# Attention with a mixture of experts: binding the first sequence's transposes, value products and early expert products behind its scores

## The chip, the cores and the metric

The kernel runs on one core of a Trainium2 chip. The metric is the device time of one execution in microseconds (us); the median of three runs stands for a kernel.

## The reference

Four sequences of 576 tokens with eight heads of 64 columns go through causal attention with a bias that decays along the sequence; the result is the input of a mixture of eight experts, whose gate is balanced in eight rounds over all tokens.

```python
scores = scale * np.matmul(q, k.transpose(0, 1, 3, 2))
cum = np.cumsum(np.maximum(s, 0.0), axis=-1)
bias = -(cum[:, :, :, None] - cum[:, :, None, :])
scores = np.where(causal, -1000000000.0, scores + np.minimum(bias, 0.0))
attn = np.exp(scores - np.max(scores, axis=-1, keepdims=True))
attn = attn / (np.sum(attn, axis=-1, keepdims=True) + 1e-09)
x = np.matmul(attn, v)                  # tokens x 512
...
P = np.exp(x @ w_gate - max)            # then 8 rounds of row and column balancing
for e in range(E):
    out += P[:, e:e + 1] * (np.maximum(x @ w1[e], 0.0) @ w2[e])
```

## The kernel before, in words

The work has two parts. The first, which the change touches, is attention; expert 0's products run between its pieces. The second, from some 340 us on, is the other seven experts, whose products are made from sums of blocks (lines 1017 to 1236).

All values are kept as a rounded high part and a remainder, so most products are made of three matmuls.

Attention goes by pairs of heads: sequence 0 has pairs 0 to 3 (heads 0 to 7), sequence 1 pairs 4 to 7, and so on. A pair has five blocks of queries, so a step of the main loop (line 722) is one pair g and one block i; sequence 0 has steps 0 to 19. The list `slots` (line 673) holds them. The work of a step is spread over four turns of the loop:

- `st0` (line 519): the scores (two matmuls into a bank, line 505, for each of the pair's heads), the search for the largest on VectorE (line 514), the exponential with its sum on ScalarE (line 546). Three banks hold scores.
- `st1` (line 555), one turn later: a small addition on ScalarE (line 561), the reciprocal on VectorE (line 565), the scaling on ScalarE (line 568).
- `st2` (line 570), two turns later: transposes on TensorE (lines 577 and 587, two banks), copies to `at` or `al` on VectorE (lines 582, 585, 588).
- `st3` (line 591), three turns later, but for blocks 0 and 1 together after block 1 and for blocks 2 to 4 together after block 4: the product with V on TensorE (line 607, one bank `pv`), its rounding on ScalarE (line 623) and its remainder on VectorE (line 624) into `xh`, the input of the experts.

The operands of a head are made by `prep_head` (line 410) from transfers of `load_head` (line 330): the high part of Q on GpSimd (line 425), that of K and a copy of Q's on VectorE (lines 426 and 429), the remainders on GpSimd (line 432 for K, line 436 for Q, in two pieces for an odd head), the rows of the bias by transfers (lines 418 and 421). Four sets of Q operands are used in turn, so head h waits for the scores of head h - 4. V of a pair is loaded by `load_v` (line 490) into two tiles used in turn.

Expert 0's weights are split on ScalarE and GpSimd (lines 110 and 111). Its products for a sequence (`g1_half`, line 141, matmuls at line 149, each half over two of the four pairs' columns; `g2_chunk`, line 170) and the gate (`gate`, line 628, matmuls at line 632) are queued two turns after the sequence's last step (line 775), and `fill` (line 696) spreads them over the next turns. Two banks `g` hold them.

The order of the program is not that of the chip's queues: a scheduler with a timeline of its own decides, engine by engine, which of the traced instructions comes next, earlier traced ones first among those that it believes to be ready. The products with V have a priority that lets them pass 4000 places (line 606). `tc.issue_after(x)` adds an edge for the instructions in its block that are on the engine of x: they stand behind x in that engine's queue. It adds no wait on a semaphore. On the chip each engine takes its queue in order.

The main loop's part that the change touches reads:

```python
for ti in range(NS + 3):
    if ti < NS:
        ...
            st0(slots[ti], j)
    if 1 <= ti <= NS:
        st1(slots[ti - 1])
    fill(ti)
    if 3 <= ti:
        pg, pi = slots[ti - 3]
        if pi == 1:
            st3(pg, (0, 1))
        elif pi == 4:
            st3(pg, (2, 3, 4))
    for j in range(2):
        if 2 <= ti < NS + 2 and j in heads(slots[ti - 2]):
            st2(slots[ti - 2], j)
```

Of the kernel before, what the change touches and what calls it, by code (L numbers as in the profile page):

```python
# [14 lines left out]
P = 128  # L15
B, H, S, D = 4, 8, 576, 64
# [7 lines left out]
KD = DM // P  # L24
# [21 lines left out]
def fused_kernel(ctx: ExitStack, tc: tile.TileContext, qT, kT, v, s, w_gate, wu, out):  # L46
    nc = tc.nc
# [10 lines left out]
    wg = const.tile([P, KD, 16], F32R, name="wg")  # L58
# [19 lines left out]
    def xcols(b, hl, k, n0, n):  # L78
        return xgroup(b)[:, hl, k, n0 - GB[b] : n0 - GB[b] + n]
# [55 lines left out]
    gps = {}  # L135
    chunk = {}

    def bank():
        return cur["g"].tile([P, 512], F32, name=cur["gt"], tag=cur["gt"])

    def g1_half(b, u, n0, n, f, half):
        w1 = wts[u, "w1"]
        if half == 0:
            gps[0] = bank()
        ps = gps[0]
        for k in (0, 1) if half == 0 else (2, 3):
            o = k * FU + f * P
            for t, (w, x) in enumerate(((0, 0), (0, 1), (1, 0))):
                nc.tensor.matmul(  # L149
                    ps[:, :n],  # L150
                    lhsT=w1[:, w, o : o + P],
                    rhs=xcols(b, x, k, n0, n),
                    start=(k == 0 and t == 0),
                    stop=(k == KD - 1 and t == 2),
                )
        if half == 1:
            hh = hpool.tile([P, TP], F32R, name="hh", tag="hh")
            hl = hpool.tile([P, TP], F32R, name="hl", tag="hl")
            nc.scalar.activation(hh[:, :n], ps[:, :n], AF.Relu)
            nc.vector.scalar_tensor_tensor(  # L160
                out=hl[:, :n],
                in0=ps[:, :n],
                scalar=0.0,
                in1=hh[:, :n].bitcast(F32),
                op0=ALU.max,
                op1=ALU.subtract,
            )
            hts[u, n0, f] = hh, hl
# [225 lines left out]
    for n in range(4):  # L394
        qa = apool.tile([P, QW], F32R, name=f"qa{n}")
# [10 lines left out]
        vtt.append(vt)  # L406

    ops = {}

    def prep_head(h):  # L410
        rq, rk = raws.pop((h, "q")), raws.pop((h, "k"))
        ka = apool.tile([P, S], F32R, name="ka", tag="ka", bufs=4)
        kb = apool.tile([D + 4, S], F32R, name="kb", tag="kb", bufs=4)
        qa, qb = qas[h % 4], qbs[h % 4]
        rows = crow_d[h : h + 1]
        at = [(0, 0, S)] if h % 2 == 0 else [(0, 0, S - D), (S - D, S, D)]
        for i, o, n in at:
            nc.sync.dma_start(
                out=qb[D : D + 4, o : o + n].bitcast(F32), in_=rows[:, 2:6, i : i + n]
            )  # L420
        nc.sync.dma_start(out=kb[D : D + 4, :].bitcast(F32), in_=rows[:, 0:4, :])
        top = D if h < H else P
        low = slice(0, D) if h < H else slice(D, P)
        for i, o, n in at:
            nc.gpsimd.tensor_copy(qa[:top, o : o + n], rq[:top, i : i + n])
        nc.vector.tensor_copy(ka, rk)
        if h < H:
            for i, o, n in at:
                nc.vector.tensor_copy(qb[:D, o : o + n], rq[:D, i : i + n])
        else:  # L430
            nc.sync.dma_start(out=qb[:D].bitcast(F32), in_=qa[:D].bitcast(F32))
        nc.gpsimd.tensor_tensor(
            out=kb[:D], in0=rk[:D], in1=ka[:D].bitcast(F32), op=ALU.subtract
        )
        for i, o, n in at:
            nc.gpsimd.tensor_tensor(
                out=qa[D:, o : o + n], in0=rq[low, i : i + n],
                in1=qa[low, o : o + n].bitcast(F32), op=ALU.subtract,
            )
        ops[h] = (ka, kb)  # L440

    def first_heads():
# [56 lines left out]

    Ts, sums, ats = {}, {}, {}  # L500

    def scores(out, h, i, cols, first, last):
        ka, kb = ops[h]
        for n, (q, k) in enumerate(((qas[h % 4], ka), (qbs[h % 4], kb))):
            nc.tensor.matmul(  # L505
                out,
                lhsT=queries(q, h, i),
                rhs=k[:, cols],
                start=(first and n == 0),
                stop=(last and n == 1),  # L510
            )
# [58 lines left out]
    def st2(t, j):  # L570

        g, i = t
        T = Ts.pop((t, j))
        nb = min(i + 1, 4)
        tr = psa.tile([P, 512], F32, name="tr", tag="tr", bufs=2)
        for c in range(nb):
            nc.tensor.transpose(  # L577
                tr[:, c * P : (c + 1) * P], T[:, c * P : (c + 1) * P], ident
            )
        if i < 4:  # L580
            at = apool.tile([P, 512], F32, name="at", tag="at", bufs=6)
            nc.vector.tensor_copy(at[:, : nb * P], tr[:, : nb * P])
        else:
            at = apool.tile([P, 5 * P], F32, name="al", tag="al", bufs=1)
            nc.vector.tensor_copy(at[:, : 4 * P], tr)
            tr = psa.tile([P, 512], F32, name="tr", tag="tr", bufs=2)
            nc.tensor.transpose(tr[:, :P], T[:, S - P : S], ident)
            nc.vector.tensor_copy(at[:, 4 * P :], tr[:, :P])
        ats[t, j] = at
# [38 lines left out]
    def gate(b, n0, n):  # L628
        ps = bank()
        for k in range(KD):  # L630
            for x in range(2):
                nc.tensor.matmul(  # L632
                    ps[:16, :n],
                    lhsT=wg[:, k, :],
                    rhs=xcols(b, x, k, n0, n),
                    start=(k == 0 and x == 0),
                    stop=(k == KD - 1 and x == 1),
                )
        lt = apool.tile([16, 384], F32, name="lt", tag="lt", bufs=2)
        nc.scalar.copy(lt[:, :n], ps[:16, :n])  # L640
        lts[n0] = lt
# [31 lines left out]
    slots = [(g, i) for g in range(B * NPAIR) for i in range(5)]  # L673
# [48 lines left out]
    for ti in range(NS + 3):  # L722
        if ti < NS:
            g, i = slots[ti]
            if i == 4 and g + 1 < NG:
                load_v(g + 1)
            for j in heads(slots[ti]):
# [3 lines that stand above are left out]
        fill(ti)  # L731
        if 3 <= ti:
            pg, pi = slots[ti - 3]
            if pi == 1:
                st3(pg, (0, 1))
            elif pi == 4:
                st3(pg, (2, 3, 4))
        for j in range(2):
            if 2 <= ti < NS + 2 and j in heads(slots[ti - 2]):
                st2(slots[ti - 2], j)  # L740
            if j == 0:
                fill(ti)
        if ti < NS and i in (1, 3) and g + 1 < NG:
            h = 2 * (g + 1) + i // 2
            prep_head(h)
            ahead = {2: (4, 5), 3: (6,), 16: ()}.get(h, (h + (3 if h < 16 else 2),))
            for hh in ahead:
                if hh < B * H:
                    load_head(hh)
        gs = (ti - 7) // 5  # L750
        if ti >= 7 and slots[ti - 7][1] == 4 and gs >= NPAIR:
            spill(*divmod(gs, NPAIR))
        if ti in (24, 28, 32, 36):
            spill(0, (ti - 24) // 4)
        if ti == 6:
            gate_weights()
        if 4 <= ti < 18:
            u, r = divmod(ti - 4, 7)
            if r in (0, 3):
                with tc.issue_after(heads_in[0].ins):  # L760
                    w_load_early(u, (r // 3,))
            if r > 2:
                w_split_early(u, r - 3)
        prep(ti)
        if ti == 66:
            for i in range(2):
                nc.gpsimd.tensor_copy(
                    xgroup(3)[:, i, :, : EDGE[1] - EDGE[0]],
                    xgroup(2)[:, i, :, GB[3] - GB[2] : GB[3] - GB[2] + EDGE[1] - EDGE[0]],
                )  # L770

        for bb in range(B):
            if ti == (bb + 1) * 20 + 2:
                if bb < B - 1:
                    for k in range(4):
                        stream.add_visit(4 * bb + k, w_load_early, w_split_early)
                else:
                    stream.flush()
                for x, (n0, n) in enumerate(EARLY[bb]):
                    at = 4 * x + 1 if bb < B - 1 else 3 * x + 1  # L780
                    stream.queue.insert(at, lambda b=bb, n0=n0, n=n: gate(b, n0, n))
                    stream.queue.insert(at + 2, lambda n0=n0, n=n, t=bb == B - 1: gate_t(n0, n, t))
# [457 lines left out]
    k = 0  # L1240
# [107 lines left out]
    for i in range(len(steps2)):  # L1348
# [6 lines left out]
        idx, o = steps2[i]  # L1355
# [46 lines left out]
```

## Time and profile before

| | |
|---|---|
| median of 3 runs | 1686.53 us (1685.39 to 1687.65) |
| the profiled execution | 1686.63 us |
| its span, first to last instruction | 1684.8 us |
| TensorE busy | 1661.1 us (99%) |
| VectorE, ScalarE, GpSimd busy | 1177.9, 833.9, 872.9 us |
| mean granted clock of TensorE | 0.994 of 2.4 GHz |

The profile is one execution on the chip. Its engines are PE (TensorE), PEld (TensorE's loads of weights), DVE (VectorE), ACT (ScalarE), POOL (GpSimd) and SP (the queue that issues most transfers). L505 is line 505 of the kernel. A row of the instructions in order of time gives the start, the duration, the engine, the line, what it writes and reads, and in brackets how long the engine was idle before it and what ended that. Matmuls overlap, and a record's end is modelled, so a busy TensorE is not always one at its peak.

### The profile page before, as it was taken

What the parts mean: (1) busy time and instruction counts of PE and PEld (TensorE: products, weight loads), DVE (VectorE), ACT (ScalarE), POOL (GpSimd) and SP (SyncE); (2) the same over time, 40 slices, a digit from 0 to 9 for tenths busy, and PEclk for the clock granted to TensorE, in tenths of its full rate; (3) what the DMA queues carried; (4) which work ended last, traced back from release to release, by engine and by line L of the source; (5) the groups of instructions that cost most, each with busy time, mean ns of one, the idle gap of its engine ahead of it and who ended that gap; (6) DMA issues with size and microseconds to landing.
All of it is one profiled execution on the core that took longest, in us unless ns stands there. A gap on an engine that the chain in (4) does not pass through costs nothing.

```text
span 1684.8 us, 31220 instructions
## 1 busy us (share of the span) xinstructions
PE 1661.1 (99%) x11149; PEld 1565.7 (93%) x11149; DVE 1177.9 (70%) x2313; ACT 833.9 (49%) x1816; POOL 872.9 (52%) x800
## 2 busy tenths in 40 slices
PE   7999999999999999999999999999999999999999
PEld 5789898988898999999899999999999999999998
DVE  7866566655866766676457777777777777777666
ACT  5976666533544444444235444444445444444443
POOL 7857867432654554454214544554554555455544
PEclk8999999999999999999999999999999999999999
DMA  6577666284876866875956666565687666666552
GB/s 181 166 203 229 205 174 198 86 310 162 297 246 215 281 214 210 286 227 180 349 181 208 187 184 191 187 189 183 191 316 248 203 188 189 187 187 184 189 186 88
DMA packets 203578, 348.88 MB, mean 207 GB/s; under 512 B 20832, under 2 KB 102752, under 8 KB 203392
## 3 DMA queue, kind: packets, MB, share of 16 engines
q1 hardware_dynamic: 202944, 345.98, 64.2%
q8 instruction: 88, 1.44, 0.4%
q10 hardware_dynamic: 480, 0.92, 0.2%
q14 instruction: 66, 0.54, 0.1%
HBM read 247.71 MB, written 94.81 MB: 203 GB/s over the span
## 4 chain that ended last, share of the span: by engine, by line
PE 91%; DVE 5%; ACT 2%; issue 1%; DMA 1%; SPq 1%; POOL 0%; ACTq 0%; DVEq 0%; POOLq 0%
PE c L1038 34%; PE zz L1159 13%; PE zz L1216 13%; PE y L1216 10%; PE g L149 4%; PE g L178 4%; PE sc L505 3%; PE pv L607 3%; PE tr L577 2%; PE c L149 2%; PE c L178 2%; DVE s L1013 1%; DVE h L253 1%; PE g L632 0%; DVE z L256 0%
## 5 line engine op out<-in xcount | busy, mean ns | idle before, releaser
L253 POOL TENSOR_TENSOR w2o<-r,w2o 128x512 fp32r<-128x512 f32 x192 | 276.7, 1462 | 279.4 <-ACT w2o L1196 274.9
L1216 PE MATMUL zz<-w2o,h 128*128 128x256 f32 x2016 | 272.9, 280 | 0.0
L1038 PE MATMUL c<-xS,w1o 128*128 128x384 f32 x1344 | 271.7, 336 | 1.1 <-ACT t L1053 0.6
L1216 PEld LDWEIGHTS zz<-w2o,h 128*128 128x128 f32 x2016 | 263.3, 188 | 0.4 <-DVE h L253 0.2
L1159 PE MATMUL zz<-w2p,h 128*128 128x512 f32 x1008 | 256.8, 391 | 0.4 <-ACT h L1001 0.4
L1002 DVE SCALAR_TENSOR_TENSOR h<-z,h 128x384 fp32r<-128x384 f32 x252 | 193.0, 772 | 66.2 <-ACT h L1001 63.6
L1001 ACT ACTIVATE h<-z 128x384 fp32r<-128x384 f32 x252 | 130.6, 525 | 207.1 <-DVE z L256 203.3
L1038 PEld LDWEIGHTS c<-xS,w1o 128*128 128x128 f32 x1344 | 227.3, 188 | 2.9 <-DVE z L256 1.6
L1013 DVE SCALAR_TENSOR_TENSOR s<-z,s 128x384 f32<-128x384 f32 x224 | 180.7, 844 | 65.7 <-ACT s L1076 62.7
L253 POOL TENSOR_TENSOR h<-s,h 128x384 fp32r<-128x384 f32 x112 | 138.2, 1242 | 163.2 <-ACT h L1009 162.4
L1159 PEld LDWEIGHTS zz<-w2p,h 128*128 128x128 f32 x1008 | 187.0, 188 | 29.6 <-ACT h L1001 0.7
L1038 PE MATMUL c<-x,w1o 128*128 128x384 f32 x1008 | 203.0, 336 | 0.0
L1216 PE MATMUL y<-w2o,h 128*128 128x256 f32 x1512 | 201.5, 280 | 0.4 <-DVE a L1142 0.3
L1216 PEld LDWEIGHTS y<-w2o,h 128*128 128x128 f32 x1512 | 194.5, 188 | 1.0 <-DVE a L1142 0.5
L256 DVE TENSOR_TENSOR z<-c,t 128x384 f32<-128x384 f32 x252 | 136.6, 549 | 69.4 <-PE c L1038 65.3
L1038 PEld LDWEIGHTS c<-x,w1o 128*128 128x128 f32 x1008 | 170.5, 188 | 0.6
L1142 DVE SCALAR_TENSOR_TENSOR a<-zz,prob,a 128x256 f32<-128x256 f32 (+1 forms) x210 | 110.5, 529 | 67.6 <-PE zz L1216 53.0
L1009 ACT CAST h<-s 128x384 fp32r<-128x384 f32 x224 | 110.9, 513 | 74.7 <-DVE s L1013 69.7
L1038 PE MATMUL c<-xS,wp 128*128 128x384 f32 x672 | 134.6, 336 | 1.4 <-DVE z L256 1.3
L1196 ACT CAST w2o<-r 128x1024 fp32r<-128x1024 f32 x98 | 102.5, 1047 | 51.9 <-PE y L1216 41.0
L1038 PEld LDWEIGHTS c<-xS,wp 128*128 128x128 f32 x672 | 118.9, 188 | 10.0 <-DVE z L256 3.1
L253 POOL TENSOR_TENSOR wp<-s,wp 128x512 fp32r<-128x512 f32 x56 | 80.4, 1436 | 82.3 <-ACT wp L928 70.5
(151 smaller groups left out, 2723.0 us busy)
## 6 DMA issues: line engine op xcount, KB each, us to landing
w1o<-w1d SPq DMA_DIRECT2D x392, 256.0 KB
w1d<-wp SPq DMA_DIRECT2D x84, 512.0 KB
r<-wu SPq DMA_DIRECT2D x70, 512.0 KB
r<-w2d SPq DMA_DIRECT2D x56, 512.0 KB
sa<-wu SPq DMA_DIRECT2D x28, 512.0 KB
w2d<-sb SPq DMA_DIRECT2D x56, 256.0 KB
wraw<-wu SPq DMA_DIRECT2D x20, 512.0 KB
xS<-xd_S SPq DMA_DIRECT2D x12, 768.0 KB
```

The source lines that it names most:

```text
L149: nc.tensor.matmul(ps[:, :n], lhsT=w1[:, w, o : o + P], rhs=xcols(b, x, k, n0, n), start=(k == 0 and t == 0), stop=(k == KD - 1 and t == 2),)
L253: (eng or nc.gpsimd).tensor_tensor(out=out, in0=a, in1=b, op=ALU.subtract)
L256: (eng or nc.gpsimd).tensor_tensor(out=out, in0=a, in1=b, op=ALU.add)
L1001: mark["a"] = nc.scalar.activation(t[:, 0], z, AF.Relu)
L1002: mark["v"] = nc.vector.scalar_tensor_tensor(out=t[:, 1], in0=z, scalar=0.0, in1=t[:, 0].bitcast(F32), op0=ALU.max, op1=ALU.subtract,)
L1009: nc.scalar.copy(t[:, 0], z)
L1013: nc.vector.scalar_tensor_tensor(out=out, in0=z, scalar=0.0, in1=other, op0=ALU.max, op1=op)
L1038: mm = nc.tensor.matmul(ps, lhsT=w[:, wl, k], rhs=x[:, xl, k], start=(fresh and k == 0 and t == 0), stop=(k == 1 and t == 2), skip_group_c ...
L1142: nc.vector.scalar_tensor_tensor(out=a, in0=ps, scalar=prob[:, c, e : e + 1], in1=a, op0=ALU.mult, op1=ALU.add)
L1159: mm = nc.tensor.matmul(zb[ci], lhsT=h[:, a, ci * P : (ci + 1) * P], rhs=w[:, b_], start=(ui == 0 and f == 0 and t == 0), stop=(ui == UPE ...
L1196: nc.scalar.copy(w[:, :, 0], r)
L1216: nc.tensor.matmul(ps, lhsT=h[:, a, ci * P : (ci + 1) * P], rhs=w[:, ui, b_], start=(fresh and ui == 0 and t == 0), stop=(ui == UPE - 1 an ...
```

## The change

Three kinds of instructions get an edge in their engine's queue; nothing is computed otherwise.

- In turns 1 to 20, the transposes of step ti - 2 and the product with V of step ti - 3 stand behind the last score of step ti - 1 on TensorE.
- For the first sequence, expert 0's first products and the gate's products stand behind the last score of step 18 on TensorE.
- On GpSimd, the copies of Q (line 425) of heads 3 to 8 stand behind the last subtraction (line 436) of the head before.

```diff
+    def behind_first(b):
+        st = ExitStack()
+        if b == 0:
+            st.enter_context(tc.issue_after(last_score[slots[18]].ins))
+        return st
+
@@ g1_half
-            for t, (w, x) in enumerate(((0, 0), (0, 1), (1, 0))):
-                nc.tensor.matmul(
...
+            with behind_first(b):
+                for t, (w, x) in enumerate(((0, 0), (0, 1), (1, 0))):
+                    nc.tensor.matmul(
...
@@ prep_head
-        for i, o, n in at:
-            nc.gpsimd.tensor_copy(qa[:top, o : o + n], rq[:top, i : i + n])
+        with ExitStack() as st:
+            if h - 1 in split_q:
+                st.enter_context(tc.issue_after(split_q[h - 1].ins))
+            for i, o, n in at:
+                nc.gpsimd.tensor_copy(qa[:top, o : o + n], rq[:top, i : i + n])
...
-            nc.gpsimd.tensor_tensor(
+            lo = nc.gpsimd.tensor_tensor(
...
+        if h < H:
+            split_q[h] = lo
@@ scores
+    last_score = {}
+
+    def behind_scores(ti):
+        st = ExitStack()
+        if 0 < ti <= 20:
+            st.enter_context(tc.issue_after(last_score[slots[ti - 1]].ins))
+        return st
+
...
-            nc.tensor.matmul(
+            last_score[h // 2, i] = nc.tensor.matmul(
                 out,
@@ gate
+                with behind_first(b):
+                    nc.tensor.matmul(
...
@@ main loop
             pg, pi = slots[ti - 3]
-            if pi == 1:
-                st3(pg, (0, 1))
-            elif pi == 4:
-                st3(pg, (2, 3, 4))
+            with behind_scores(ti):
+                if pi == 1:
+                    st3(pg, (0, 1))
+                elif pi == 4:
+                    st3(pg, (2, 3, 4))
...
-                st2(slots[ti - 2], j)
+                with behind_scores(ti):
+                    st2(slots[ti - 2], j)
```

## Rows read from the trace of the kernel before

**Rows 1.** The page, busy time, share of the span and count of each engine.

```profile
PE 1661.1 (99%) x11149; PEld 1565.7 (93%) x11149; DVE 1177.9 (70%) x2313; ACT 833.9 (49%) x1816; POOL 872.9 (52%) x800
```

**Rows 2.** Busy time by stretch: length, engines' busy time (instructions), TensorE's clock, transfers.

```profile
core 0: us, PE busy (x) PEld busy (x) DVE busy (x) ACT busy (x) POOL busy (x), PEclk, DMA share, GB/s
0.00:42.00 42.00, 29.87 (x179) 24.84 (x179) 30.28 (x83) 22.41 (x64) 30.70 (x51) 0.81 0.68 180
42.00:84.00 42.00, 39.69 (x372) 32.75 (x372) 34.32 (x137) 40.81 (x126) 33.59 (x35) 0.95 0.58 165
84.00:126.00 42.00, 42.00 (x371) 37.54 (x371) 27.12 (x88) 32.20 (x92) 21.57 (x22) 1.00 0.71 205
```

**Rows 3.** The same view, columns as above, from 26.5 to 81.2 us.

```profile
26.50:33.60 7.10, 5.18 (x57) 4.37 (x56) 3.07 (x6) 0.04 (x2) 5.79 (x5) 0.76 0.84 237
33.60:41.60 8.00, 4.84 (x27) 3.59 (x27) 7.68 (x25) 7.14 (x24) 5.39 (x7) 0.88 0.53 146
...
56.60:69.40 12.80, 11.81 (x119) 9.45 (x118) 11.18 (x45) 12.20 (x38) 11.88 (x13) 1.00 0.58 158
69.40:81.20 11.80, 10.96 (x117) 9.21 (x115) 10.58 (x42) 11.48 (x37) 7.42 (x9) 1.00 0.72 204
```

**Rows 4.** Who waited for whom, first 200 us: total us, times, longest us.

```profile
ACT xh L623 <- PE pv L607: 9.1, 4, 7.1
```

**Rows 5.** TensorE's instructions in order of time, 25 to 90 us.

```profile
27.29 0.63 PE L577 MATMUL tr<-ident,T 128*128 128x128 f32 x4 [0.54 <-DVE at L582]
...
29.63 1.34 PE L607 MATMUL pv<-al,vt 128*64 128x64 f32 x20 [0.47 <-DVE al L588]
30.75 2.76 PE L607 MATMUL pv<-at,vt 128*64 128x128 f32 x28
33.44 0.33 PE L505 MATMUL sc<-ka,qa 128*128 128x128 f32 x1
...
41.59 0.45 PE L505 MATMUL sc<-ka,qa 128*128 128x128 f32 x1 [2.92 <-DVE mn L514]
...
78.72 1.70 PE L607 MATMUL pv<-at,vt 128*64 128x128 f32 x28
...
85.21 1.60 PE L149 MATMUL g<-xh,w 128*128 128x256 f32 x12
```

**Rows 6.** GpSimd's instructions in order of time, around 23 us.

```profile
22.80 0.88 POOL L425 CAST qa<-rx 64x576 fp32r<-64x576 f32 x1
23.76 1.70 POOL L436 TENSOR_TENSOR qa<-rawq,qa 64x512 fp32r<-64x512 f32 x2
```

**Rows 7.** ScalarE's instructions in order of time, 15 to 38 us.

```profile
15.69 0.90 ACT L568 ACTIVATE T<-T,rec 128x256 f32<-128x256 f32 x2
...
34.25 0.40 ACT L546 ACTIVATE T<-T,mn 128x128 f32<-128x128 f32 x1 [0.32 <-DVE mn L514]
34.56 0.19 ACT L546 ACTIVATION_READ_ACCUMULATOR T<-T,mn 128x1 f32 x1
...
34.78 0.29 ACT L561 ACTIVATE sm<-sm,guard 128x2 f32<-128x2 f32 x1
34.98 0.49 ACT L546 ACTIVATE T<-T,mn 128x256 f32<-128x256 f32 x1
...
37.61 0.68 ACT L568 ACTIVATE T<-T,rec 128x128 f32<-128x128 f32 x2
```

**Rows 8.** SP's queue in order of time, around 35 us.

```profile
35.28 0.41 SPq L495 DMA_DIRECT2D vt<-v  x1
```

**Rows 9.** TensorE's busy time (instructions) in one stretch: line 149, then line 632.

```profile
26.50:61.50 35.00, 1.71 (x6) 1.19 (x6) 0.85 0.59 170
...
26.50:61.50 35.00, 0.63 (x4) 0.38 (x4) 0.85 0.59 170
```

**Rows 10.** VectorE's instructions in order of time, 23 to 85 us.

```profile
23.62 0.43 DVE L426 CAST ka<-rx 128x576 fp32r<-128x576 f32 x1
...
38.44 2.08 DVE L426 CAST ka<-rawk 128x576 fp32r<-128x576 f32 x1
...
84.44 0.21 DVE L624 TENSOR_TENSOR xh<-pv,xh 128x64 fp32r<-128x64 f32 x1
```

More of the change, by code (lines that the diff above doesn't have):

```diff
@@ L147, in g1_half @@
             o = k * FU + f * P
-            for t, (w, x) in enumerate(((0, 0), (0, 1), (1, 0))):
-                nc.tensor.matmul(
[L150 to L155, printed above, removed]
+            with behind_first(b):
+                for t, (w, x) in enumerate(((0, 0), (0, 1), (1, 0))):
+                    nc.tensor.matmul(
+                        ps[:, :n],
+                        lhsT=w1[:, w, o : o + P],
+                        rhs=xcols(b, x, k, n0, n),
+                        start=(k == 0 and t == 0),
+                        stop=(k == KD - 1 and t == 2),
+                    )
         if half == 1:
@@ L408, in fused_kernel @@
     ops = {}
+    split_q = {}
     def prep_head(h):
@@ L631, in gate @@
             for x in range(2):
[L632 to L638, printed above, removed]
+                with behind_first(b):
+                    nc.tensor.matmul(
+                        ps[:16, :n],
+                        lhsT=wg[:, k, :],
+                        rhs=xcols(b, x, k, n0, n),
+                        start=(k == 0 and x == 0),
+                        stop=(k == KD - 1 and x == 1),
+                    )
         lt = apool.tile([16, 384], F32, name="lt", tag="lt", bufs=2)
```

## The prediction

> **What bounds it now.** I read the page's totals first, then busy time by stretch, then who waited for whom, then each engine's instructions in order of time around the largest wait. TensorE is busy for 1661.1 of 1684.8 us [rows 1], so all that another order can win is the 23.7 us in which it is not, and what a lower clock costs. The first 42 us hold 42.00 - 29.87 = 12.13 us of that and the next 42 us 42.00 - 39.69 = 2.31 us; from 84 to 126 us there is none, at a clock of 1.00 [rows 2]. So the change, which touches the first sequence's attention, works in the one stage that has much to give, and behind about 84 us TensorE is full: what is won or lost before is handed on to the end, and what is moved across that line is paid in full.
>
> Up to about 81 us ScalarE and VectorE set the pace. From 56.6 to 81.2 us ScalarE is busy for 12.20 of 12.80 and 11.48 of 11.80 us, VectorE for 11.18 and 10.58 [rows 3]. Against that stands the stretch from 26.5 to 33.6 us: ScalarE is busy for 0.04 of 7.10 us, VectorE for 3.07 [rows 3]. The list of waits names it: ScalarE's longest, 7.1 us, is for the product with V [rows 4]. The order on TensorE shows why. It does the transposes of step 4 from 27.29 us, then 20 and 28 instructions of the product with V for steps 2 to 4 (29.63 to 33.5 us), and only at 33.44 us the score of head 3 for step 5 [rows 5]. That score could have gone earlier: GpSimd's last piece of head 3 (the subtraction at 23.76 us, 1.70 us long) is over at 25.46 us [rows 6]. So scores that feed the two pacing engines stand in line behind 3.9 us of products that nobody needs yet. No measurement of this kernel tells a difference under 0.2% (3.4 us) from none.
>
> **The change part by part.**
>
> Steps bound behind scores. Step n's transposes must follow the scores of step n+1, and the product with V of steps 2 to 4 must follow the scores of step 6. I went through TensorE's order of the first sequence with this rule; it is broken in one place only, by the transposes of step 4 and the 48 products behind them [rows 5]. Elsewhere the binding asks for what is there. Here the score of step 5 (head 3) and both of step 6 come ahead of the 48 products. TensorE reaches them at about 27.3 us, 1.8 us after head 3 is complete, so it needn't wait for it. ScalarE then has work in its gap: exponentials of 0.40, 0.49 and 0.49 us, three reads of a sum at 0.19, two small additions at 0.29, scalings of 0.68 and 0.90 us [rows 7], together 4.1 us. These ten overlap by 0.09 us each (the first begins at 34.25 us, lasts 0.40 us, and the next begins at 34.56 us), which leaves 3.2 us. Step 7's first score should pass as well, since TensorE otherwise stands still before the products (0.47 us before 29.63 us, 0.54 us before 27.29 us [rows 5]); that is one exponential more, 0.6 us by the next larger size after 0.40 and 0.49 us, an estimate. I take 3.8 us, close to what the binding secures, because the products keep their priority and will follow closely. Bounds: all 7.1 us of the gap, if the scores up to step 9 pass too; nothing, if VectorE, which has copies and casts of its own until 29.6 us, serves the early scores no sooner than now. TensorE has room: its gaps are 1.92 us in the first stretch, then 3.16, 0.99 and 0.84 us in the others, 6.91 us together [rows 3].
>
> What the moved instructions drag along. The 48 products move back by four to six score instructions (0.33 us for the one at 33.44 us [rows 5]), under 2 us. ScalarE's rounding and VectorE's remainder of them move too; their reader, expert 0's product, comes 50 us later: nothing. On SP's queue the load of V for pair 2 waits for the last of these products and is issued at 35.28 us [rows 8], with the rows of head 6 behind it. Those wait for the last score of pair 1 anyway; without that cover the loads are up to 2 us late, for scores 20 us away: nothing.
>
> GpSimd's chain (for heads 3 to 8, the copy stands behind the last subtraction of the head before). Now head 4's copy (22.80 us, 0.88 us) goes ahead of head 3's subtraction [rows 6]; it will go behind it. Head 3 is complete 0.9 us earlier, which counts for nothing, as TensorE arrives at 27.3 us. Heads 4 and 5 need the same instructions on an engine that is busy for 5.79 of the 7.10 us [rows 3], and are wanted when pair 2's scores begin, at 41.59 us now [rows 5] and near 38 us then: nothing. Should a chained head have to wait for a transfer, it delays the next head by the copy and the subtraction, 0.88 + 1.70 us, still less than that cover.
>
> Expert 0's products and the gate, behind step 18. Up to its score at about 61.5 us, six product instructions and four of the gate run [rows 9]; these ten move behind it. Twelve such products take 1.60 us at 85.21 us [rows 5], 0.13 us each, so ten take 1.3 us. Between 61.5 us and the point where TensorE fills up it has 0.84 us of gap in one stretch and about half of the other's 0.99 us [rows 3], the same 1.3 us, so I cost them at nothing. If that cover is gone they cost all 1.3 us, because whatever crosses into the filled stretch is added to the end.
>
> The sum: -3.8 us, with ends at -7.1 us (whole gap back, products hidden) and +1.3 us. The profiled execution took 1686.63 us around its span of 1684.8 us, 0.1 us from the median of 1686.53 us, so it stands for the median: 1686.5 - 3.8 = **1682.7 us**.
>
> **The rivals.**
>
> The gap opens again (no change). ScalarE gets its work early but runs dry a little later, because VectorE can't follow: it has the casts for heads 6 and 7 in between, one of which takes 2.08 us at 38.44 us, where the same cast takes 0.43 us at 23.62 us [rows 10]. Then half of the 3.8 us or nothing is won and up to 1.3 us of products is paid: -1.9 to +1.3 us, 1684.6 to 1687.8 us. For it: both engines are nearly full later on. Against: VectorE leaves 1.62 us of 12.80 and 1.22 of 11.80 [rows 3], so it can catch up. The Trainium skill, "SBUF — State Buffer", Who interferes with whom, says that casts in a two-port mode and GpSimd's instructions lock each other out for a whole instruction. By that rule every cast that is pulled beside GpSimd's work could grow as the long one did, and the sum would fall to this rival's; the 2.08 us agree, the 0.43 us do not, and GpSimd was at work beside both.
>
> Everything comes back (much faster). Steps 7 to 9 pass as well, and a part of TensorE's next gap, 3.16 us from 33.6 to 41.6 us [rows 3], goes too: 7.1 + 0.9 = 8 us, 1678.5 us. Against: the products' priority.
>
> TensorE blocks at expert 0's products (slower). Released in one go behind step 18, they stand where the scheduler believes pair 3's columns to be ready. On the chip the remainder of pair 3 is written at 84.65 us, 4.2 us after the product with V that it needs (78.72 + 1.70 us) [rows 5, 10]; a product placed right behind the latter holds up all of TensorE for that time. Two banks hold the early products, so it can happen twice: 2 x 4.2 + 1.3 - 3.8 = +5.9 us, 1692.4 us. It decides against the change once such waits exceed 3.8 us. For it: the scheduler took head 3 to be late here when it was not, so its clock is off by several us. Against: at 85.21 us the twelve products run without a wait [rows 5]. The Trainium skill, "TensorE: Matmul & The Clock Gate", The mechanism, says that matmuls start and end strictly in program order; the trace agrees in that the score at 33.44 us came after the 48 products though its operands had been ready for 8 us.
>
> The change does not do what it says. If the scheduler already kept the edges, nothing would move; rows 5 exclude that for step 4, but a reshuffle of the 1600 us behind, where TensorE still loses 23.7 - 14.4 = 9.3 us, could cancel the gain. It gives the first rival's time and is counted there.
>
> **How the numbers follow.** Forecast (-2 to -6 us) 0.48; the gap opens again or a reshuffle eats the gain 0.29; everything comes back 0.08; TensorE blocks 0.15. Of the forecast's 0.48 some 0.36 lie beyond -3.4 us; with the 0.08 that makes 0.44 faster. The forecast's other 0.12, the first rival's 0.29 and 0.02 of a short block make 0.43 the same; 0.13 slower. The range leaves out the far half of a block and the fast end's last part: 1678.3 to 1690.5 us; the likeliest case's own is 1680.5 to 1684.5 us.
>
> **What would show it.** Right: the score of head 3 for step 5 near 27 us and both of step 6 ahead of the 48 products; ScalarE's wait of 7.1 us gone; pair 2's scores near 38 us, TensorE full near 80 us; head 4's copy behind head 3's subtraction; no product of expert 0 ahead of step 18's score. Wrong: a new wait of TensorE for a rounding or for GpSimd between 25 and 85 us, ScalarE idle again before 45 us, or 14.4 us of gaps in TensorE up to 84 us as now.

## The result, and the profile after

The changed kernel took 1698.26 us (median of 6 runs, 1696.76 to 1700.59) against 1687.09 us for the kernel before beside it: a ratio of 1.0073, 95% interval 1.0062 to 1.0084. It is 11.2 us **slower**. The forecast was 1682.7 us, and the range ended at 1690.5 us.

The page's totals come first, then TensorE's time by stretch (columns as in [rows 2]).

```profile
PE 1664.9 (98%) x11149; PEld 1571.0 (93%) x11149; DVE 1188.9 (70%) x2313; ACT 836.0 (49%) x1816; POOL 871.6 (51%) x800
```

```profile
0.00:42.00 42.00, 29.32 (x176) 24.86 (x177) 32.11 (x77) 22.87 (x64) 29.86 (x49) 0.82 0.70 187
42.00:84.00 42.00, 36.26 (x298) 30.83 (x298) 32.40 (x116) 34.66 (x106) 28.49 (x30) 0.86 0.49 139
84.00:126.00 42.00, 39.29 (x329) 34.67 (x328) 25.53 (x87) 31.58 (x91) 20.27 (x21) 0.92 0.69 199
...
60.00:70.00 10.00, 8.94 (x72) 8.04 (x74) 6.86 (x26) 7.59 (x25) 8.31 (x8) 0.66 0.54 145
...
90.00:100.00 10.00, 7.39 (x36) 6.26 (x34) 5.78 (x17) 5.44 (x20) 5.46 (x5) 0.66 0.86 234
```

The span is 1695.0 us, 10.2 us more than before. TensorE stands still for 1695.0 - 1664.9 = 30.1 us where it was 23.7 [rows 1]: 6.4 us. The same 11149 instructions keep it busy 3.8 us longer, because the granted clock averages 0.66, so partly the lower level of 1.2 GHz, in two stretches with new gaps (60 to 70 and 90 to 100 us) in which it was 1.00, 2.4 GHz throughout, before. All of the new standstill lies in the first sequence's attention: up to 126 us the gaps are 126 - 104.87 = 21.13 us against 14.44 [rows 2], and from there to the end TensorE loses about what it did (9.0 us, 9.3 before).

The list of waits up to 130 us names who waited; the row with VectorE's copy in it (line 603, the transposed scores) was 4.2 us at 5 times before.

```profile
PE tr L598 <- DVE at L603: 14.0, 9, 4.9
```

```profile
ACT T L567 <- DVE mn L535: 18.7, 14, 3.9
```

Both wait for VectorE; the second was 12.0 us at 9 times before. TensorE's order of time shows what was forecast and what was not:

```profile
26.26 0.74 PE L526 MATMUL sc<-ka,qa 128*128 128x128 f32 x2
...
30.78 0.63 PE L526 MATMUL sc<-ka,qa 128*128 128x512 f32 x1
...
31.77 1.34 PE L628 MATMUL pv<-al,vt 128*64 128x64 f32 x20
32.89 2.07 PE L628 MATMUL pv<-at,vt 128*64 128x128 f32 x28
...
41.81 0.66 PE L598 MATMUL tr<-ident,T 128*128 128x128 f32 x2 [4.88 <-DVE at L603]
42.41 0.45 PE L526 MATMUL sc<-ka,qa 128*128 128x128 f32 x1
...
60.16 0.52 PE L598 MATMUL tr<-ident,T 128*128 128x128 f32 x3 [3.25 <-DVE at L603]
```

The scores of steps 5, 6 and 7, and one of step 8, stand ahead of the 48 products with V, as the prediction's part on the bound steps said [rows 5]. But pair 2 begins at 42.41 us, not near 38, behind two transposes that wait for VectorE's copy. VectorE, around the 4.88 us wait:

```profile
25.22 2.60 DVE L440 CAST qb<-rx 64x512 fp32r<-64x512 f32 x2
...
36.39 3.39 DVE L437 CAST ka<-rx 128x576 fp32r<-128x576 f32 x1 [0.31 <-DMA rawk<-kT]
39.70 0.46 DVE L440 CAST qb<-rx 64x576 fp32r<-64x576 f32 x1
40.08 0.15 DVE L586 RECIPROCAL rec<-sm 128x2 f32<-128x2 f32 x1
40.16 1.31 DVE L440 CAST qb<-rawq 64x64 fp32r<-64x64 f32 x1
41.39 0.27 DVE L603 COPY at<-tr 128x128 f32<-128x128 f32 x1
```

The cast that took 0.43 us in one place and 2.08 us in another [rows 10] takes 3.39 us here, and a cast of 64 columns takes 1.31 us, three times the 0.46 us of one nine times its size just before. The row minima, the reciprocals and the copy for which TensorE waits are queued behind them. GpSimd in the same stretch works without a pause:

```profile
36.37 0.66 POOL L436 CAST qa<-rx 64x576 fp32r<-64x576 f32 x1 [4.32 <-PE sc L526]
36.99 2.47 POOL L111 TENSOR_TENSOR w<-wraw,w 128x512 fp32r<-128x512 f32 x2
39.41 0.43 POOL L711 CAST wg<-wgr 128x32 fp32r<-128x32 f32 x1
39.91 1.50 POOL L443 TENSOR_TENSOR kb<-rx,ka 64x576 fp32r<-64x576 f32 x1
...
48.16 0.78 POOL L436 CAST qa<-rawq 64x512 fp32r<-64x512 f32 x2
...
56.01 1.26 POOL L447 TENSOR_TENSOR qa<-rawq,qa 64x512 fp32r<-64x512 f32 x1
...
58.79 0.41 POOL L447 TENSOR_TENSOR qa<-rawq,qa 64x64 fp32r<-64x64 f32 x1
```

The long cast ends at 39.78 us, inside GpSimd's small one (39.41 to 39.84 us), after three longer instructions of GpSimd; the other ends at 41.47 us, just after GpSimd's subtraction (41.41 us). The three lower rows are head 7's: its last subtraction is over at 59.2 us, and its first score stands at 64.7 us, behind transposes and products of pair 2; head 6's is at 55.8 us (before: 56.6 and 56.9 us for the two). So two suspects stood after this reading: the **port** that VectorE's casts and GpSimd share (theory B in the expectations below), and the **late head** on GpSimd's chain (theory A). The Trainium skill, "SBUF — State Buffer", Who interferes with whom, gives the port pair as an exclusive lock, and that a reduction never takes it on trn2; in e5 (below) a cast grows by 1.10 us, most of one GpSimd subtraction of 1.39 us, and a reduction by nothing, 0.752 and 0.751 us, so both agree here.

### The profile page after: what moved, and what is told of

Its sections match the earlier page's. It is cut to its first block, busy times and chain, and to the rows that moved or that the text cites. A ratio compares the mean times of both kernels' runs of the same rounds, so it can differ in the third digit from the quotient of the medians.

```text
span 1695.0 us, 31226 instructions
## 1 busy us (share of the span) xinstructions
PE 1664.9 (98%) x11149; PEld 1571.0 (93%) x11149; DVE 1188.9 (70%) x2313; ACT 836.0 (49%) x1816; POOL 871.6 (51%) x800
## 4 chain that ended last, share of the span: by engine, by line
PE 91%; DVE 4%; issue 1%; ACT 1%; POOL 1%; DMA 1%; SPq 0%; DVEq 0%; ACTq 0%; POOLq 0%
PE c L1062 34%; PE zz L1183 13%; PE zz L1240 13%; PE y L1240 10%; PE g L156 4%; PE g L185 4%; PE sc L526 3%; PE pv L628 3%; PE tr L598 2%; PE c L156 2%; PE c L185 2%; DVE s L1037 1%; DVE h L260 1%; PE g L654 0%; DVE ka L437 0%
## 5 line engine op out<-in xcount | busy, mean ns | idle before, releaser
L1220 ACT CAST w2o<-r 128x1024 fp32r<-128x1024 f32 x98 | 102.5, 1047 | 52.3 <-PE y L1240 41.4
```

The lines of the kernel that those rows point to most:

```text
L1220: nc.scalar.copy(w[:, :, 0], r)
```

## The experiments

Each ran beside the kernel before on the same chip; differences are of medians. The kernel before was at 1685.2 to 1685.6 us beside them, except for 1684.7 us beside e13 and e14. Half an interval is 0.09 to 0.13%, 1.5 to 2.1 us, so these runs tell smaller differences than the 3.4 us of the prediction. Some expectations say 9.2 and 6.9 us for what the table has as 9.3 and 6.8 us.

| run | what it is | us | against before | ratio, 95% interval |
|---|---|---|---|---|
| e1 | both bindings on TensorE, no chain | 1692.06 | +6.8 | 1.0036 (1.0023 to 1.0048) |
| e2 | GpSimd's chain alone | 1694.52 | +9.3 | 1.0054 (1.0042 to 1.0067) |
| e3 | steps behind scores alone | 1687.44 | +2.2 | 1.0013 (1.0004 to 1.0022) |
| e4 | expert 0 and gate alone | 1685.35 | +0.1 | 1.0000 (0.9992 to 1.0009) |
| e6 | whole change, casts as reductions | 1685.53 | 0.0 | 1.0002 (0.9993 to 1.0011) |
| e7 | before, casts as reductions | 1687.20 | +1.7 | 1.0009 (1.0000 to 1.0018) |
| e8 | whole change, head 7 not chained | 1688.45 | +2.9 | 1.0017 (1.0009 to 1.0026) |
| e9 | before, head 7's first score held | 1686.95 | +1.5 | 1.0010 (1.0001 to 1.0019) |
| e10 | chain alone, casts as reductions | 1680.12 | -5.3 | 0.9970 (0.9959 to 0.9982) |
| e11 | both bindings, casts as reductions | 1688.46 | +3.0 | 1.0018 (1.0009 to 1.0027) |
| e12 | chain's link for head 7 alone | 1683.34 | -2.1 | 0.9988 (0.9979 to 0.9997) |
| e13 | e2, head 6's casts as reductions | 1690.78 | +6.1 | 1.0036 (1.0023 to 1.0048) |
| e14 | whole change, the same for head 6 | 1689.96 | +5.3 | 1.0026 (1.0015 to 1.0037) |
| e15 | e2, heads 6 and 7 as reductions | 1688.46 | +3.3 | 1.0017 (1.0008 to 1.0026) |
| e16 | whole change, the same for 6 and 7 | 1689.76 | +4.6 | 1.0028 (1.0018 to 1.0037) |

**Parts alone (e1 to e4).** Each part is switched off in the changed kernel with one line:

```diff
 # GpSimd's chain off (e1, e3, e4)
-            if h - 1 in split_q:
+            if False:
 # steps behind scores off (e2, e4)
-        if 0 < ti <= 20:
+        if False:
 # expert 0 and gate off (e2, e3)
-        if b == 0:
+        if False:
```

> The change without GpSimd's chain (heads 3 to 8 free again, both TensorE bindings kept). Theory A (the chain makes head 7 complete at 59.2 us instead of 50.0 us and pushes pair 3's scores behind pair 2's products): the loss of 11 us goes and the early scores' gain of up to 4 us shows, 1683 to 1688 us. Theory B (the bindings on TensorE put VectorE's casts beside GpSimd's work, where the port holds them up): still 1692 us or more.

> Only GpSimd's chain, no binding on TensorE. Theory A: the scores of pair 3's second head stand behind pair 2's transposes and product with V again, so 1693 to 1700 us, at or above the whole change. Theory B: about the time of before, 1685 to 1689 us.

> Only the transposes and products with V bound behind scores. Theory A: below before by what the prediction worked out, 1682 to 1686 us. Theory B: 1692 us or more. Theory C (expert 0's products held back behind step 18 cost TensorE's filled stretch 1.3 us or a block): this one is faster than the run that also binds them by 1.3 us or more.

> Only expert 0's first products and the gate bound behind step 18. Theories A and B: within 2 us of before, 1685 to 1689 us. Theory C: slower by 1.3 us (ten products moved into the filled stretch) up to 8 us (two blocks).

Neither theory had these four right: e1 came out as B said (1692 us or more), e2 as A said (1693 to 1700 us), e3 as neither. The gap between e3 and e1 that theory C asked for is there (4.6 us), but not its price in e4. The chain alone costs most, 9.3 us; the products and the gate alone cost nothing. The bound scores cost 2.2 us, although they do what was forecast at first. In order: a row of TensorE, one of VectorE and one of ScalarE in e3.

```profile
38.52 0.47 PE L526 MATMUL sc<-ka,qa 128*128 128x128 f32 x1 [2.48 <-DVE mn L535]
```

```profile
40.91 1.38 DVE L440 CAST qb<-rawq 64x64 fp32r<-64x64 f32 x1
```

```profile
42.93 1.34 ACT L589 ACTIVATE T<-T,rec 128x512 f32<-128x512 f32 x2 [3.29 <-DVE rec L586]
```

Pair 2 begins at 38.52 us, 3.1 us earlier than before and where the prediction had it. Then five casts for heads 6 and 7 stand on VectorE between 38.38 and 42.29 us, ScalarE waits 3.29 us for a reciprocal behind them, and pair 3 begins at 56.8 us, no earlier than before (56.6 us). The gap opened again one pair later.

In e2 the lock is at its plainest: VectorE, then GpSimd, then TensorE's longest wait.

```profile
37.51 0.45 DVE L437 CAST ka<-rx 128x576 fp32r<-128x576 f32 x1
37.88 4.87 DVE L440 CAST qb<-rx 64x576 fp32r<-64x576 f32 x1
42.68 1.24 DVE L440 CAST qb<-rawq 64x64 fp32r<-64x64 f32 x1
```

```profile
37.70 0.79 POOL L436 CAST qa<-rx 64x576 fp32r<-64x576 f32 x1
38.46 1.25 POOL L111 TENSOR_TENSOR w<-wraw,w 128x512 fp32r<-128x512 f32 x1
39.67 0.20 POOL L711 CAST wg<-wgr 128x32 fp32r<-128x32 f32 x1
39.83 1.39 POOL L443 TENSOR_TENSOR kb<-rx,ka 64x576 fp32r<-64x576 f32 x1
41.19 2.69 POOL L111 TENSOR_TENSOR w<-wraw,w 128x512 fp32r<-128x512 f32 x2
```

```profile
PE pv L628 <- DVE at L603: 6.9, 1, 6.9
```

A cast that takes 0.45 us just before takes 4.87 us while GpSimd goes from one instruction into the next, and TensorE waits 6.9 us for the copy behind it. The kernel before was not free of this: its five casts for heads 6 and 7 took 0.86, 0.44, 0.44, 2.08 [rows 10] and 0.19 us, 4.0 us in all, against 6.0 us in the changed kernel and 7.6 us in e2.

**The port by itself (e5), and the casts off it (e6, e7).** e5 is a small program that computes nothing of the reference: it times VectorE's instructions alone and beside a run of GpSimd's subtractions. e6 and e7 write both casts as a maximum over one element, which gives the same values:

```diff
-        nc.vector.tensor_copy(ka, rk)
+        nc.vector.tensor_reduce(out=ka, in_=rk.unsqueeze(2), axis=AX.X, op=ALU.max)
...
-                nc.vector.tensor_copy(qb[:D, o : o + n], rq[:D, i : i + n])
+                nc.vector.tensor_reduce(out=qb[:D, o : o + n],
+                    in_=rq[:D, i : i + n].unsqueeze(2), axis=AX.X, op=ALU.max)
```

> A program of its own that computes nothing of the reference: VectorE's cast of 128x576 (as for K's high part) six times alone, then six times while GpSimd subtracts 64x576 tiles without a break, then the same cast done as a reduction over one element, alone and beside the subtractions, then copies out of PSUM beside them. Theory B (a fast VectorE cast and a GpSimd instruction exclude each other, and GpSimd, when it follows itself, keeps the port): the cast is 0.43 us alone and at least 1.4 us, or up to the whole run of subtractions, beside GpSimd; the reduction is 0.6 to 0.7 us and the copy 0.67 us both alone and beside it. If B is wrong all keep their times.

> The whole change, with VectorE's casts of K and Q (13 and 8 in the first 110 us) done as reductions over one element: slower by 0.2 us each when nothing stands in the way. Theory B (port): the long casts go and with them VectorE's 5 to 8 us of blocked time, 1686 to 1692 us. Theory A (the chain's late head 7 alone): 1695 to 1700 us, unless the scheduler's order also changes, which the trace has to show.

> The kernel before, with the same replacement of the casts and nothing else. Theory B: before loses 0.65 + 1.63 + 1.1 us in its three long casts and pays some 0.2 us for each of the others, so within 3 us of before either way, 1682 to 1689 us. Theory A: says nothing; 1685 to 1690 us.

Groups of e5's instructions (count, then busy time and mean ns): the cast alone (line 88) and beside GpSimd (line 92), the reduction alone (95) and beside (99), and GpSimd's subtraction beside casts (lowb) and beside reductions (lowd).

```profile
L92 DVE CAST cb<-rk 128x576 fp32r<-128x576 f32 x6 | 9.3, 1556 | 0.2
...
L95 DVE TENSOR_REDUCE cc<-rk 128x576 fp32r<-128x576 f32 x6 | 4.5, 752 | 0.2
L99 DVE TENSOR_REDUCE cd<-rk 128x576 fp32r<-128x576 f32 x6 | 4.5, 751 | 0.2
...
L88 DVE CAST ca<-rk 128x576 fp32r<-128x576 f32 x6 | 2.8, 460 | 2.3 <-DMA rk<-kT 2.1
```

```profile
L79 POOL TENSOR_TENSOR lowb<-ra,rb 64x576 fp32r<-64x576 f32 x12 | 17.3, 1442 | 0.9
L79 POOL TENSOR_TENSOR lowd<-ra,rb 64x576 fp32r<-64x576 f32 x12 | 16.7, 1390 | 0.9
```

The cast grows from 0.46 to 1.56 us, by most of one subtraction of GpSimd (1.39 us), while the subtraction grows by 4%. The reduction takes 0.75 us in both places. In this program no cast waited for more than one instruction; the 3.39 and 4.87 us of the kernels were not reproduced by it. With reductions the whole change is level with before (e6), so all of its loss is gone; the same replacement without the change gains nothing (e7, +1.7 us).

The replacement does more than free the port, however: it changes the scheduler's order. In e7, which has none of the three edges, the score of head 3 for step 5 already stands ahead of the 48 products (30.23 us), and pair 2 waits all the same:

```profile
25.91 0.36 PE L526 MATMUL sc<-ka,qa 128*128 128x128 f32 x1
...
39.93 0.47 PE L526 MATMUL sc<-ka,qa 128*128 128x128 f32 x1 [4.22 <-DVE mn L535]
```

So the early scores are no sure gain even with reductions in place of these casts, whose own price of 0.3 us each at 128x576 is in e7 too; the 2.2 us of e3 are not shown to be the port's.

**The late head (e8, e9, e12).** e8 is the whole change with head 7's copy unchained. e9 goes the other way: the kernel before, with head 7's first score bound where the changed kernel's schedule has it. e12 keeps one link of the chain.

```diff
 # e8: the changed kernel
+            if h - 1 in split_q and h not in (7,):
 # e12: the changed kernel, both bindings off
+            if h - 1 in split_q and h == 7:
 # e9: the kernel before, in st0; last_pv holds the last product with V
+            with ExitStack() as st:
+                if (g, i, j) == (3, 0, 1):
+                    st.enter_context(tc.issue_after(last_pv[2, 0].ins))
                 scores(sc[:, :n], 2 * g + j, i, slice(0, n), True, True)
```

> The whole change, but head 7's copy is not chained behind head 6's subtraction (heads 3 to 6 and 8 stay chained). Theory A: pair 3's second score comes 6 us earlier than in the whole change (near 58 us in place of 64.7), 1687 to 1693 us. Theory B: the casts stay blocked, 1695 us or more.

> The kernel before, with one edit: the second score of pair 3 (head 7's first) is bound behind the products with V of pair 2's first two tiles, where the changed kernel's schedule puts it; GpSimd's and VectorE's work is untouched. Theory A (late head: the chain delays head 7, so its first score stands behind pair 2's transposes and products, and TensorE, which goes in order, starves both pacing engines): that score at 62 us or later instead of 56.9 us, and +5 to +9 us, 1691 to 1695 us. Theory B (port: the chain costs because VectorE's casts are locked out by GpSimd): the order by itself is cheap, -1 to +1.5 us.

> One link of GpSimd's chain alone: head 7's copy waits for head 6's subtraction; all else as before. Theory A (late head): head 7's subtraction is over after 55 us (50.0 us before), its first score comes 3 us or more after head 6's, and the time rises by 4 to 9 us. Theory B (port): GpSimd's work is the same apart from the order of two pieces, no cast is longer than 2.1 us, and the time stays within +1.5 us.

Freeing head 7 brings its first score back to 56.9 us and 8.3 of the 11.2 us, though a cast still waits (3.19 us at 38.18 us). Yet the late score alone costs 1.5 us (e9: 59.6 us instead of 56.9), and the link alone makes the kernel 2.1 us faster (e12: head 7 complete at 53.4 us, its score at 56.9 us). But neither makes the score as late as the 64.7 us of the changed kernel: theory A's conditions (62 us in e9, a head complete after 55 us in e12) were not met, so what so late a score costs by itself is not shown. Nor is e8, where A's time came true and B's 1695 us or more did not, a test of the score alone. Two casts at pair 3 changed as well; first the whole change, then e8:

```profile
56.15 1.45 DVE L437 CAST ka<-rawk 128x576 fp32r<-128x576 f32 x1
57.51 1.51 DVE L437 CAST ka<-rx 128x576 fp32r<-128x576 f32 x1
```

```profile
56.89 0.59 DVE L437 CAST ka<-rawk 128x576 fp32r<-128x576 f32 x1
57.41 0.48 DVE L437 CAST ka<-rx 128x576 fp32r<-128x576 f32 x1
```

In the whole change they stand beside head 7's subtractions (56.01 to 59.20 us), and TensorE's wait of 3.25 us at 60.16 us is for a copy behind them. In e8 those subtractions are over by 48.7 us, and no wait of TensorE between 50 and 66 us is over 0.7 us. The chain's late head thus works in part through the port.

**Chain against port (e10, e11).** With the same two replacements:

> GpSimd's chain alone (neither binding on TensorE), with VectorE's casts of the heads' columns written as reductions over one element, which were not held up beside GpSimd (0.753 us alone and beside). The chain alone cost 9.2 us with plain casts. Theory A (late head): most of it stays, +5 to +9 us. Theory B (port): it is gone, -1 to +2 us.

> Both bindings on TensorE without GpSimd's chain, casts as reductions. With plain casts these bindings cost 6.9 us. Theory A (late head; the chain is a cost of its own): it lies below the whole change with reductions (1685.5 us), at 1681 to 1684.5 us, and below the kernel before: the gain that was forecast. Theory B (port): without the port the chain costs nothing, so it comes out within 1.5 us of 1685.5 us.

The chain costs 9.3 us with plain casts (e2) and **gains** 5.3 us with reductions (e10); with both bindings beside it the chain costs 11.17 - 6.84 = 4.3 us with plain casts (e1 to the whole change; by the ratios, 1.0036 and 1.0073, 6 us) and gains 3.0 us with reductions (e11 to e6). Theory A, by which most of the cost should have stayed in e10, falls as an account of the chain; so does its forecast for e11. Theory B has the direction right and the sizes wrong: e10 lies 4.3 us below its range of -1 to +2 us, and e11 3.0 us above the 1685.5 us that it gave to within 1.5 us. The order that came with the reductions is in both. e10's casts beside GpSimd, which works without a pause from 33.59 to 40.72 us, and its stretches:

```profile
33.61 0.75 DVE L437 TENSOR_REDUCE ka<-rx 128x576 fp32r<-128x576 f32 x1
34.28 0.73 DVE L440 TENSOR_REDUCE qb<-rx 64x576 fp32r<-64x576 f32 x1
```

```profile
0.00:42.00 42.00, 32.87 (x206) 28.40 (x208) 33.10 (x100) 28.29 (x80) 31.75 (x52) 0.81 0.70 185
42.00:84.00 42.00, 39.93 (x390) 33.48 (x387) 35.27 (x127) 38.75 (x123) 30.80 (x35) 0.98 0.67 193
```

TensorE's gaps up to 84 us are 9.13 + 2.07 = 11.2 us, against 14.44 before and 18.4 after. e10 is the fastest kernel of the study and beats both.

**How much of it is the port (e13 to e16).** A reduction is priced differently by the scheduler, so e10's order of instructions differs as well. These four replace the casts of head 6, or of heads 6 and 7, and leave the others. They keep the order where it matters: in e13 and e15 GpSimd's order is that of e2 up to 53 us and TensorE's up to 50 us (times of e15), but for one product of expert 0; in e14 and e16 both are those of the whole change, up to 56 us and 45 us.

```diff
+        if h == 6:                  # e13, e14; h in (6, 7) in e15, e16
+            nc.vector.tensor_reduce(out=ka, in_=rk.unsqueeze(2), axis=AX.X, op=ALU.max)
+        else:
             nc.vector.tensor_copy(ka, rk)
...
```

> GpSimd's chain alone, with head 6's casts alone written as reductions. In the chain alone (9.2 us slower than before) these were the casts that took 4.87 and 1.24 us. The schedule puts head 7's first score behind six products with V of pair 2, as in the changed kernel. Port: they take 0.75 us and less, VectorE wins about 5 us at 38 us, and the time is 0 to 3 us above before at most. Order (the schedule, not the port): the time stays 5 to 9 us above before.

> The whole change with head 6's casts alone written as reductions. In the whole change (11.2 us slower than before) these took 3.39 and 1.31 us, against 0.75 us and less as reductions. Port: 3.3 us come back there, and with them what queued behind, 4 to 9 us in all: +2 to +7 us against before. Order: unchanged, +9 to +12 us.

> GpSimd's chain alone, with the casts of heads 6 and 7 written as reductions (the others plain). TensorE's order stays that of the chain alone up to pair 2, and at pair 3 head 7's first score still stands behind products with V of pair 2. Port: no cast of VectorE is over 1 us between 36 and 45 us, and the loss of 9.2 us falls to +2 us or less. Order: at least +5 us stay, as with head 6's casts alone (6.1 us).

> The whole change with the casts of heads 6 and 7 written as reductions. Port: the loss of 11.2 us falls to +3 us or less. Order: it stays at +5 us or more, as with head 6's casts alone (5.3 us).

In e13 the lock moved to the next plain cast, of 64 columns:

```profile
39.77 0.73 DVE L444 TENSOR_REDUCE qb<-rx 64x576 fp32r<-64x576 f32 x1
40.42 3.28 DVE L446 CAST qb<-rawq 64x64 fp32r<-64x64 f32 x1
```

The chain's loss goes 9.3, 6.1, 3.3 and -5.3 us as no head, head 6, heads 6 and 7, and all heads are taken off the port; the whole change's goes 11.2, 5.3, 4.6 and 0.0 us. With the order kept, heads 6 and 7 bring back 6.0 us of the chain's loss (e2 to e15) and 6.6 us of the whole change's (to e16). The ends lie clear of each other; neighbours do not always (9.3 to 6.1, 6.1 to 3.3 and 5.3 to 4.6 us within the intervals, and e14's runs spread from 1685.9 to 1693.8 us). That much is the port's, as far as the order was kept. The last step, to all heads, changes the order as well and is not the port's alone. The port theory's bounds held in e14 only: e13 came out 3.1 us above them, within what an order would have left, and e15 and e16 1.3 and 1.6 us above them. What stays in them (in both, a pair of casts of 64x512 before pair 2 still takes 2.6 us; in e15 head 7's first score is at 62.4 us) isn't divided between port and order; in e16 the binding of expert 0's products is also at work (below).

## Why the prediction was wrong

**The failed step** is the part on GpSimd's chain: "Heads 4 and 5 need the same instructions on an engine that is busy ... nothing", with 0.88 + 1.70 = 2.58 us as its worst case, under the time until pair 2's scores begin. The chain alone cost 9.3 us, with one wait of TensorE of 6.9 us in pair 2; added behind both bindings it cost 4.3 us. The step counted what GpSimd's instructions delay through their data, and the cover it named was time to the next reader. It left out who else uses what GpSimd uses. The new order set the casts of heads 6 and 7 on VectorE beside another run of GpSimd's instructions (36.4 to 41.4 us); two of the three casts there waited out what was running, and the copies and minima behind them waited too. Taking the casts of these two heads off the port, with the order kept, brought back 6 us of the loss; for the rest the cause is open.

**The gain of 3.8 us** was right in its first step and in place, and was given back. The order changed first where the prediction said, though not only there: the score of head 3 moved from 33.44 [rows 5] to 26.26 us, and two transposes came to stand ahead of pair 2 (41.81 us). ScalarE's wait fell from 7.1 [rows 4] to 3.85 us, but a new one of 3.72 us, for a reciprocal behind the long casts, stands at 40.27 us; in e3 pair 2 began 3.1 us earlier, and all of it was gone at pair 3. That is the first rival, "VectorE can't follow", with the casts for heads 6 and 7 as its place; it came out at +2.2 us (e3), beyond its end of +1.3 us. Whether that rival needs the lock is not shown: e7, with reductions for casts and TensorE's order that of e3 up to pair 2 (but for one score), is 1.7 us slower than before. For the chain, the row of 2.08 us beside one of 0.43 us [rows 10] was the right evidence, and the prediction set it aside because GpSimd was at work beside both. The 0.43 us cast began as GpSimd passed from one instruction to the next (22.80 + 0.88 = 23.68 us [rows 6]), which reads as timing, not as a sign that the port is free. The rule that the prediction weighed there (the Trainium skill, "SBUF — State Buffer", Who interferes with whom) was the better guide.

**Expert 0's products at nothing** holds in the order of before (e4, +0.1 us). It doesn't hold everywhere, and this term failed second: e1 is 4.6 us above e3, and e6 5.3 us above e10, where the binding of scores changes nothing, as TensorE's order up to 58 us is the same in both but for these products, the gate and one score. In e10 six of these products run between 34.2 and 46.3 us; in e6 the first is at 58.95 us. Why that costs 5 us and not the 1.3 us of the instructions isn't settled; the schedules differ in more than these products.

**The other rivals.** TensorE did not block at expert 0's products: they first run at 72.64 us, and TensorE's longest wait at one of them or at the gate is 1.21 us, at 91.69 us. The price of 1692.4 us lay on the right side for another reason. The sum over parts failed too: 2.2, 0.1 and 9.3 us make 11.6, near the 11.2 measured, but two of the parts alone make 6.8 us (e1) where their sum is 2.3.

**The range** ended at 1690.5 us because no case in it gave the chain a price of its own, and because the lock was priced as a gain lost, not as a new wait.

What stays open: how the 8.3 us that freeing head 7 brings back divide between the late score and the two casts beside its subtractions, what makes up the 4.6 us left in e16, and why casts waited through three to five instructions of GpSimd in the kernels, but through one in e5.

## What to carry to other kernels

Before GpSimd's instructions are moved, look at which of VectorE's casts from SBUF to SBUF, the on-chip memory, will stand beside them, and at what is queued behind those: a cast that appears with 0.4 and with 2 us in one trace is the sign. A reduction in the cast's place costs 0.3 us more at 128x576 and, for two heads' casts, brought back 6 us (e2 to e15). It also moves the scheduler's order, so it can do harm (e7, +1.7 us) or more good (e10, 14.6 us below e2) than the port accounts for. A hint to the scheduler moves work that it doesn't name; run each hint alone and with the others before the sum is believed.

## What the runs showed of the hardware

In e5 the lock was lopsided: beside GpSimd a cast took 1.56 us for 0.46 us, and the subtraction 1.44 us for 1.39 us. In the kernels either engine could be the one that waits. In a run of different instructions of GpSimd a cast of VectorE waited for several: 4.87 us in e2, 3.39 us after. The other way round, in the kernel before, GpSimd's copy stood beside a run of VectorE's casts (36.92 to 38.51 us), of which one is shown:

```profile
37.45 1.54 POOL L425 CAST qa<-rawq 64x512 fp32r<-64x512 f32 x1
38.07 0.44 DVE L429 CAST qb<-rx 64x576 fp32r<-64x576 f32 x1
```

The same copy took 0.60 us in e3 (at 38.12 us); there, beside three casts of 0.44 to 0.48 us, GpSimd's copy of 64 columns took 1.01 us (at 39.66 us) for 0.23 us in the kernel before. In e5 a copy of 128x512 out of PSUM, TensorE's banks, took 0.69 us beside GpSimd, much as where GpSimd stands still (0.67 us at 51.55 us of the changed kernel), and a reduction within SBUF 0.75 us; neither waited for it.
